# One core, linear attention and a gated layer: the same work in another hand-written order of all engines

## The chip, the core and the metric

The kernel runs on one core of one Trainium2 chip. Five engines work side by side, each through its own queue in order: TensorE (PE in the profile, its weight loads PEld), VectorE (DVE), ScalarE (ACT), GpSimd (POOL) and SyncE (SP, which here only issues DMAs). The metric is the device time of one execution in microseconds, as the median of several runs. The median of the kernel before is 104.37 us over 3 runs (104.37 to 105.62).

## The reference

Two stages. First, causal linear attention with decay `lam` per head, in blocks, for 4 batches, 8 heads, 768 positions and 64 channels. Its output is laid out as 3072 tokens by 512 features. Then a gated ("highway") layer on it:

```python
intra = einsum('bhic,bhjc->bhij', qb, kb) * Dmask      # Dmask: lam ** (i-j), causal
intra = einsum('bhij,bhjd->bhid', intra, vb)
inter = einsum('bhid,bhde->bhie', qb * lam_pow, kv_state)
out[:, :, sl] = intra + inter
kv_state = lam_block * kv_state + einsum('bhsd,bhse->bhde', kb * rev_pow, vb)
...
x = out.transpose(0, 2, 1, 3).reshape(B * S, H * D)
H = maximum(x @ w_h, 0); T = sigmoid(x @ w_t + b_t)
return T * H + (1 - T) * x
```

Inputs and output are float32.

## The kernel before

The kernel works in 12 super-blocks `n` of 256 positions, three to a batch. The decay is taken into the operands: q is multiplied by powers of `lam`, v by inverse powers, so that the mask is only 0 and 1 and the states simply add up within a batch. All products are in bf16.

The whole order is a list of tokens, `PLAN`, written out in the source. A loop reads it from left to right; each token calls one small function that issues the instructions of one step, and every engine's queue gets its instructions in the order in which the tokens stand. Semaphores between engines come from the data: a step waits for what it reads, and for the last readers of the buffer that it overwrites. `@` names the engine of a step, `=` the PSUM banks (seven, 0 to 6, and one for the state sums). The steps, with `n` the super-block, `b` one of its two halves of 128 positions, `e` the even or odd heads:

- `Lk`, `Lq`, `Lv`: load half of k, q or v (256 KB each, issued on SP, lines 221 and 224); `W.w.g`: half of a weight matrix (w=1 is the gate's `w_t`, w=0 `w_h`; line 235); `WC`: a quarter of it to bf16.
- `CK`: k to bf16 (tile kb). `CQ`: q times powers (qb, line 249). `CV`: v times powers (vs, line 255). A last number of 2 means both halves at once.
- `TK`, `TQ` (super-blocks 0 to 2, line 267) and `T.n` (from 3 on, 32 products, line 275): k and q turned by TensorE into PSUM. `EK`, `EQ`, `FK`, `FQ`: the copies of these to SBUF (kT, qT); a `T.n` is followed by four.
- `S.0`, `U.0.b`: scores and states of super-block 0 (lines 295, 300). `SS.n.e`: scores of the heads `e`, with states of the half `1-e` in between. `KE.n.b`: the copy of the state sums to SBUF (ss). The next states must wait for it.
- `M`: mask, from PSUM to SBUF (DVE, line 352), four for each n. `I`: queries times states (line 368). `A`: masked scores times v (line 374), into the same banks (bo). `D.n.b`: attention output to bf16 (xT), the input of the second stage.
- `BP`: the bias, copied into a bank ahead of the gate product. `F.n.b.1`: gate product (bt, line 404), `F.n.b.0`: the other product (bh, line 404); four matrix instructions each, called a block here. `TX.n`: xT turned back (bx, line 398). `G`: sigmoid (ACT, line 413). `X`: (gate - 1) times x (DVE, w, line 424). `H`: relu times gate (DVE, y, line 418). `Y`: total (ob, line 431). `ST`: store.
- `BS`, `B`, `BC`: the bias, split and broadcast. `PT`: ScalarE's table for the sigmoid (line 479). `Z`: an idle product of 256 columns that keeps TensorE busy at the start (line 461).

A copy is issued at line 113 on ScalarE and at line 115 on the others, whatever step it belongs to, so groups at these lines are told apart by their tiles. Buffers rotate: three for each of the loaded tiles, three or four for kb, qb, vs, kT, qT and ss, five for the output.

Of the kernel before, what the change touches and what calls it, by code (L numbers as in the profile page):

```python
# [27 lines left out]
G.1.0.2@ACT BP.1.1.2@DVE=3 TX.1.2=5 CK.3.2@ACT SS.2.1=26 KE.2.0@ACT M.2.1.1@DVE M.2.1.0@DVE F.0.0.1.2 BP.0.1.2@ACT=4
Lv.4.1 F.1.1.1.2 G.1.1.2@ACT Lq.5.1 Lv.4.0 Lk.5.0 CQ.3.2@POOL T.3=62 FQ.3.1@ACT FQ.3.0@ACT M.2.0.0@DVE WC.0.0.0@ACT
X.1.0.2@DVE WC.0.0.1@DVE I.2=13 A.2.1 A.2.0 F.0.1.1.2 Lq.5.0 FK.3.0@ACT FK.3.1@DVE CV.3.2@POOL SS.3.1=26 D.2.0@ACT  # L30
X.1.1.2@DVE WC.0.1.0@DVE BP.2.0.2@DVE=1 G.0.0.2@ACT WC.0.1.1@POOL F.1.1.0.2=5 F.1.0.0.2=0 KE.3.0@ACT D.2.1@ACT
M.3.1.0@DVE CQ.4.2@POOL TX.0.2=2 H.1.1.2@DVE Y.1.1.2@POOL H.1.0.2@DVE Y.1.0.2@DVE CK.4.2@POOL F.0.0.0.2=3 H.0.0.2@DVE
Lk.5.1 X.0.0.2@DVE BP.2.1.2@ACT=5 F.2.1.1.2 G.0.1.2@ACT G.2.1.2@ACT Lv.5.0 Lq.6.0 Lk.6.0 Y.0.0.2@POOL SS.3.0=40 Lq.6.1
M.3.1.1@DVE X.0.1.2@DVE CV.4.2@POOL T.4=35 CQ.5.2@POOL Lv.5.1 KE.3.1@ACT CK.5.2@POOL F.2.0.1.2 M.3.0.0@DVE FK.4.0@ACT
Lk.6.1 TX.2.2=6 Lq.8.0 M.3.0.1@DVE Lv.6.0 FK.4.1@ACT X.2.1.2@DVE FQ.4.1@ACT Lv.6.1 G.2.0.2@ACT X.2.0.2@DVE F.2.0.0.2=2
H.2.0.2@DVE I.3=40 A.3.1 Lq.7.0 FQ.4.0@ACT SS.4.1=51 M.4.1.0@DVE KE.4.0@ACT A.3.0 Y.2.0.2@POOL M.4.1.1@DVE
BP.3.1.2@ACT=2 F.0.1.0.2=3 H.0.1.2@DVE D.3.1@ACT F.2.1.0.2=6 H.2.1.2@DVE T.5=51 FQ.5.0@ACT Y.2.1.2@DVE Y.0.1.2@POOL
FK.5.0@ACT Lk.8.1 Lq.8.1 SS.4.0=03 FQ.5.1@ACT KE.4.1@ACT Lq.7.1 F.3.1.1.2 CK.6.2@ACT FK.5.1@DVE I.4=65 M.4.0.1@DVE
A.4.1 SS.5.0=13 M.4.0.0@DVE CQ.6.2@POOL D.3.0@ACT Lk.8.0 M.5.0.0@DVE A.4.0 D.4.0@DVE M.5.0.1@DVE D.4.1@ACT F.3.1.0.2=0
G.3.1.2@ACT H.3.1.2@DVE CV.5.2@POOL Lk.7.1 BP.3.0.2@ACT=4 CV.6.2@POOL TX.3.2=1 T.6=56 FQ.6.1@ACT SS.5.1=23 M.5.1.0@DVE  # L40
BP.4.0.2@ACT=0 F.3.0.1.2 FQ.6.0@DVE F.4.0.1.2 FK.6.1@ACT FK.6.0@DVE CQ.8.2@POOL KE.5.0@ACT G.4.0.2@ACT CQ.7.2@POOL
I.5=62 Lk.7.0 Lv.7.0 A.5.0 M.5.1.1@DVE A.5.1 SS.6.1=53 X.3.1.2@DVE G.3.0.2@ACT X.3.0.2@DVE CK.7.2@POOL M.6.1.0@DVE
F.3.0.0.2=0 H.3.0.2@DVE Lq.9.1 BP.4.1.2@ACT=4 F.4.1.1.2 M.6.1.1@DVE D.5.0@ACT KE.6.0@ACT SS.6.0=16 Y.3.1.2@POOL
D.5.1@DVE CK.8.2@ACT Lv.7.1 M.6.0.0@DVE T.8=50 G.4.1.2@ACT Lq.9.0 KE.6.1@ACT Lv.9.0 T.7=34 FK.7.1@ACT Lk.9.0
FK.7.0@ACT FK.8.1@ACT F.4.1.0.2=2 Lk.9.1 FQ.7.1@ACT FQ.7.0@DVE FQ.8.1@ACT F.4.0.0.2=1 M.6.0.1@DVE Lv.8.1 CV.7.2@POOL
H.4.1.2@DVE BP.5.1.2@ACT=2 TX.4.2=3 H.4.0.2@DVE X.4.0.2@DVE X.4.1.2@DVE I.6=64 Lv.8.0 A.6.0 Y.3.0.2@POOL FK.8.0@DVE
SS.7.1=10 M.7.1.1@DVE Y.4.1.2@POOL F.5.1.1.2 M.7.1.0@DVE ST.1 FQ.8.0@ACT F.5.1.0.2=3 Lk.10.0 G.5.1.2@ACT KE.7.0@ACT
H.5.1.2@DVE Lk.11.0 A.6.1 D.6.1@DVE SS.8.0=50 M.8.0.1@DVE M.8.0.0@DVE Lv.9.1 D.6.0@ACT SS.7.0=21 M.7.0.0@DVE
F.5.0.0.2=3 CK.9.2@POOL KE.7.1@DVE BP.5.0.2@ACT=6 F.5.0.1.2 Lq.10.0 BP.6.0.2@ACT=4 Lv.10.0 F.6.0.1.2 CQ.9.2@POOL
G.5.0.2@ACT Lq.10.1 BP.6.1.2@ACT=6 H.5.0.2@DVE Lk.10.1 G.6.0.2@ACT CV.8.2@POOL Y.4.0.2@POOL TX.5.2=0 X.5.1.2@DVE  # L50
Y.5.1.2@POOL T.9=52 FQ.9.1@ACT ST.4 Lv.10.1 FK.9.1@ACT SS.8.1=34 KE.8.0@ACT M.7.0.1@DVE FQ.9.0@DVE F.6.1.1.2
M.8.1.1@DVE CV.9.2@POOL F.6.1.0.2=1 M.8.1.0@DVE G.6.1.2@ACT H.6.1.2@DVE I.8=24 FK.9.0@ACT CQ.10.2@POOL I.7=63 A.7.0
A.7.1 A.8.1 SS.9.1=51 D.7.0@ACT X.5.0.2@DVE M.9.1.0@DVE Y.5.0.2@POOL KE.9.0@DVE A.8.0 D.7.1@ACT TX.6.2=0 X.6.1.2@DVE
F.6.0.0.2=6 M.9.1.1@DVE BP.7.0.2@ACT=3 F.7.0.1.2 D.8.0@ACT BP.7.1.2@ACT=2 TX.7.2=5 Lq.11.1 D.8.1@ACT BP.8.1.2@ACT=4
H.6.0.2@DVE G.7.0.2@ACT X.6.0.2@DVE X.7.0.2@DVE CK.10.2@POOL F.7.1.1.2 CV.10.2@POOL T.10=16 SS.9.0=03 FK.10.0@DVE
Lq.11.0 ST.0 FQ.10.0@ACT Y.6.1.2@POOL CQ.11.2@POOL G.7.1.2@ACT Y.6.0.2@POOL Lk.11.1 M.9.0.1@DVE F.8.1.1.2 KE.9.1@DVE
F.7.0.0.2=1 F.7.1.0.2=2 G.8.1.2@ACT M.9.0.0@DVE H.7.0.2@DVE I.9=34 H.7.1.2@DVE A.9.1 A.9.0 FQ.10.1@ACT X.7.1.2@DVE
FK.10.1@ACT SS.10.1=06 M.10.1.0@DVE F.8.1.0.2=1 D.9.1@ACT BP.9.1.2@ACT=2 ST.2 D.9.0@ACT KE.10.0@DVE F.9.1.1.2
BP.8.0.2@ACT=4 G.9.1.2@ACT H.8.1.2@DVE Lv.11.1 M.10.1.1@DVE SS.10.0=50 KE.10.1@ACT M.10.0.1@DVE CK.11.2@POOL T.11=31
FK.11.1@DVE FK.11.0@ACT Lv.11.0 CV.11.2@POOL Y.7.0.2@POOL FQ.11.1@ACT M.10.0.0@DVE ST.6 ST.5 TX.8.2=2 X.8.1.2@DVE  # L60
F.8.0.1.2 FQ.11.0@ACT Y.7.1.2@POOL I.10=60 G.8.0.2@ACT A.10.0 A.10.1 D.10.1@ACT X.8.0.2@DVE SS.11.0=15 M.11.0.0@DVE
D.10.0@ACT SS.11.1=34 BP.10.1.2@ACT=0 M.11.0.1@DVE M.11.1.1@DVE ST.3 TX.9.2=2 X.9.1.2@DVE Y.8.1.2@POOL BP.9.0.2@ACT=6
F.8.0.0.2=1 H.8.0.2@DVE Y.8.0.2@POOL M.11.1.0@DVE ST.7 F.9.1.0.2=5 F.9.0.1.2 G.9.0.2@ACT KE.11.0@ACT H.9.1.2@DVE
Y.9.1.2@DVE F.10.1.1.2 G.10.1.2@ACT TX.10.2=4 F.9.0.0.2=1 X.9.0.2@DVE I.11=36 A.11.1 A.11.0 BP.10.0.2@ACT=5
H.9.0.2@DVE Y.9.0.2@POOL ST.9 D.11.1@DVE F.10.0.1.2 G.10.0.2@ACT ST.8 X.10.1.2@DVE F.10.1.0.2=0 D.11.0@DVE
H.10.1.2@DVE X.10.0.2@DVE F.10.0.0.2=2 BP.11.0.2@ACT=1 F.11.0.1.2 G.11.0.2@ACT TX.11.0=6 H.10.0.2@DVE X.11.0.2@DVE
F.11.0.0.2=3 H.11.0.2@DVE BP.11.1.0@ACT=0 TX.11.1=4 Y.10.1.2@POOL BP.11.1.6@ACT=2 F.11.1.1.6 BP.11.1.5@DVE=5
# [452 lines left out]
```

## Time and profile before

| what | value |
|---|---|
| median of 3 runs | 104.37 us |
| profiled execution | 104.44 us, of which the span is 102.7 us |
| mean granted TensorE clock | 0.997 |
| read from HBM, written | 20.97 MB, 6.29 MB |
| loads of k, q, v on SP | 72, of 256 KB, median 5.5 to 5.7 us to landing |
| DMA shares of the span's 16 engines, main queue | 80.6% |
| longest waits of SP for totals, ahead of stores | 26.2 us in 5 |

The span runs from the first instruction to the last of one profiled execution; its own time has 1.7 us around it. DMA is full from about 2 to 60 us, and has room after that. The waits of SP for totals lie in the second half of the span, where few loads are left behind them.

### The profile page before, as it was taken

To read this page: it belongs to the slowest core of one execution; us is meant where nothing else is said; L and a number is where in the kernel's file an instruction comes from. 1 tells how busy PE (TensorE), PEld (TensorE's weight loads), DVE (VectorE), ACT (ScalarE), POOL (GpSimd) and SP (SyncE) were. 2 spreads that over 40 slices of the span, in tenths; PEclk is the share of its full clock that TensorE was granted. 3 is DMA by queue.
4 is the path that set the end of the run, shared out by engine and by line. 5 is a ranking of instruction groups with operands and counts; after the bars stand their busy time and mean duration, and the time that the engine had idled before them with its cause. 6 is when DMAs were issued, how large, how long until landed. Compare 5 with 4: busy or idle time off the path is not lost.

```text
span 102.7 us, 4320 instructions
## 1 busy us (share of the span) xinstructions
PE 90.0 (88%) x1834; PEld 58.5 (57%) x1853; DVE 86.2 (84%) x159; ACT 69.8 (68%) x125; POOL 76.7 (75%) x69
## 2 busy tenths in 40 slices
...
GB/s 18 259 316 352 361 372 382 377 348 387 351 347 351 284 293 339 318 337 328 293 265 358 345 344 105 6 206 288 343 341 59 238 374 208 10 0 198 211 286 125
DMA packets 33485, 27.54 MB, mean 268 GB/s; under 512 B 1465, under 2 KB 26425, under 8 KB 33466
## 3 DMA queue, kind: packets, MB, share of 16 engines
q1 hardware_dynamic: 33168, 27.14, 80.6%
...
HBM read 20.97 MB, written 6.29 MB: 265 GB/s over the span
## 4 chain that ended last, share of the span: by engine, by line
PE 66%; ACT 11%; DMA 6%; DVE 5%; SPq 4%; issue 3%; POOL 2%; ACTq 0%; POOLq 0%
PE bt L404 19%; PE bh L404 18%; PE bs L295 8%; DMA qf<-in_q_dram 6%; PE bx L398 5%; PE bo L374 5%; PE btr L275 5%; ACT kT L113 3%; ACT qT L113 3%; PE bo L368 3%; SPq L224 3%; PE kv L300 2%; POOL qb L249 2%; SPq L221 2%; DVE y L418 1%
## 5 line engine op out<-in xcount | busy, mean ns | idle before, releaser
L352 DVE TENSOR_TENSOR m<-bs,tri 128x512 bf16<-128x512 f32 x48 | 31.5, 684 | 2.7 <-PE bs L295 1.6
L431 POOL TENSOR_TENSOR ob<-y,w 128x512 f32<-128x512 bf16 (+1 forms) x21 | 23.7, 1136 | 10.3 <-DVE w L424 3.0
L404 PEld LDWEIGHTS <-xT 128*128 128x128 bf16 x208 | 18.0, 98 | 17.4
L255 POOL TENSOR_TENSOR vs<-vf,pow_v 128x1024 bf16<-128x1024 f32 (+1 forms) x12 | 22.0, 1836 | 7.8 <-DMA vf<-in_v_dram 7.8
L404 PE MATMUL bh<-w_b,xT 128*128 128x512 bf16 (+2 forms) x95 | 23.1, 361 | 0.7 <-issue 0.3
L404 PE MATMUL bt<-w_b,xT 128*128 128x512 bf16 (+2 forms) x94 | 22.7, 361 | 1.1 <-issue 0.8
L249 POOL TENSOR_TENSOR qb<-qf,pow_q 128x1024 bf16<-128x1024 f32 x11 | 20.9, 1907 | 3.0 <-DMA qf<-in_q_dram 3.0
L413 ACT ACTIVATE g<-bt 128x512 f32<-128x512 f32 (+2 forms) x26 | 14.5, 564 | 10.6 <-PE bt L404 10.3
L424 DVE SCALAR_TENSOR_TENSOR w<-g,bx 128x512 bf16<-128x512 f32 (+2 forms) x26 | 16.5, 640 | 1.9 <-ACT g L413 1.9
L295 PE MATMUL bs<-qT,kT 64*64 64x128 bf16 x384 | 14.2, 218 | 2.6 <-ACT qT L113 1.2
L418 DVE SCALAR_TENSOR_TENSOR y<-bh,g 128x512 bf16<-128x512 f32 (+1 forms) x21 | 14.1, 673 | 0.4 <-PE bh L404 0.2
L295 PEld LDWEIGHTS <-kT 64*64 64x64 bf16 x384 | 11.4, 106 | 5.3 <-issue 3.6
L113 ACT ACTIVATE bt<-b_bc 128x512 f32<-128x512 f32 (+2 forms) x22 | 12.5, 577 | 1.2 <-DVE y L418 1.0
L113 ACT ACTIVATE qT<-btr 128x512 bf16<-128x512 bf16 x15 | 8.7, 604 | 4.0 <-DVE kT L115 2.7
L113 ACT ACTIVATE xT<-bo 128x512 bf16<-128x512 f32 x16 | 9.4, 601 | 2.9 <-PE bo L374 2.9
L300 PE MATMUL kv<-vs,kb 64*64 64x64 bf16 x320 | 9.4, 197 | 0.8 <-ACT ss L113 0.7
L113 ACT ACTIVATE ss<-kv 128x512 bf16<-128x512 f32 x14 | 8.4, 601 | 1.6 <-PE bs L295 1.6
L374 PE MATMUL bo<-m,vs 64*64 64x128 bf16 x384 | 8.6, 219 | 0.7 <-DVE m L352 0.7
L300 PEld LDWEIGHTS <-kb 64*64 64x64 bf16 x320 | 7.6, 107 | 1.0 <-issue 0.9
L398 PEld LDWEIGHTS <-xT 128*128 128x128 bf16 x96 | 6.2, 98 | 2.9 <-issue 0.4
L374 PEld LDWEIGHTS <-vs 64*64 64x64 bf16 x384 | 6.3, 106 | 2.3 <-issue 1.1
L398 PE MATMUL bx<-id,xT 128*128 128x128 bf16 x96 | 7.5, 219 | 0.1
...
## 6 DMA issues: line engine op xcount, KB each, us to landing
...
```

The costliest lines, as they stand in the source:

```text
L113: A.activation(dst, src, AF.Copy)
L249: ENG[eng].tensor_tensor(new(("qb", n), [128, Q, 2, D])[:, :, es].rearrange("p j e d -> p e j d"), in0=get("qf", n)[:, es].rearrange("p e ...
L255: ENG[eng].tensor_tensor(new(("vs", n), [128, H, J, D])[:, heads(p)], in0=get("vf", n)[:, heads(p)].rearrange("p h (j d) -> p h j d", j=J) ...
L295: T.matmul(get("s", n, e, hp // 2)[half(b), hp % 2, j, :], lhsT=get("kT", n)[half(e), hp, j, half(b)], rhs=get("qT", n)[half(e), hp, b * C ...
L300: T.matmul(kv[half(e), hp, half(e)], lhsT=get("kb", n)[half(b), j, 2 * hp + e, :], rhs=get("vs", n)[half(b), 2 * hp + e, j, :], start=firs ...
L352: V.tensor_tensor(new(("m", n, e, u), [128, 2, J, C]), in0=get("s", n, e, u), in1=tri[:, None].to_broadcast([128, 2, J, C]), op=ALU.mult)
L374: T.matmul(get("o", n, b)[half(e), hp, :], lhsT=get("vs", n)[half(b), 2 * hp + e, j, :], rhs=get("m", n, e, hp // 2)[half(b), hp % 2, j, : ...
L398: T.transpose(t[:, i, j, :], get("xT", n)[:, j, b * C:(b + 1) * C], id128)
L404: T.matmul(t, lhsT=get("xT", n)[:, j, b * C:(b + 1) * C], rhs=w_b[w][:, j, z], start=(j == 0 and not w), stop=(j == KC - 1), skip_group_ch ...
L418: V.scalar_tensor_tensor(y, in0=get("h", n, b, p), scalar=0.0, in1=get("g", n, b)[:, z], op0=ALU.max, op1=ALU.mult)
L424: V.scalar_tensor_tensor(new(("w", n, b), [C, DM])[:, z], in0=get("g", n, b)[:, z], scalar=1.0, in1=x.rearrange("p j f -> p (j f)")[:, z], ...
L431: ENG[eng].tensor_tensor(o, in0=y, in1=get("w", n, b)[:, z], op=ALU.subtract)
```

## The change

Only `PLAN` is replaced: no function, no buffer count and no tile. The steps are the same, with two more `Z` (34 for 32). What is another: the order on every queue, the banks, and the engine of some steps. Counts by engine that differ:

| step | before | after |
|---|---|---|
| CQ, both halves | POOL 11 | POOL 10, DVE 1 |
| CV, both halves | POOL 11 | POOL 10, DVE 1 |
| CK, both halves | POOL 6, ACT 5 | POOL 5, ACT 6 |
| CK, one half | ACT 1, DVE 1 | ACT 2 |
| EK, both halves | ACT 2 | ACT 1, DVE 1 |
| EQ, one half | DVE 2 | DVE 1, ACT 1 |
| FK | ACT 12, DVE 6 | ACT 9, DVE 9 |
| FQ | ACT 15, DVE 3 | ACT 13, DVE 5 |
| KE | ACT 14, DVE 6 | ACT 16, DVE 4 |
| D | ACT 16, DVE 8 | ACT 19, DVE 5 |
| WC | POOL 5, DVE 2, ACT 1 | POOL 4, DVE 3, ACT 1 |
| BP, 512 wide | ACT 20, DVE 3 | ACT 19, DVE 4 |
| BP of quarter 5 of 11.1 | DVE | ACT |
| Y of 11.1, 256 wide / quarter 6 | POOL / DVE | DVE / POOL |

`U.0.0`, the first states, stands ahead of both `S.0` on TensorE. `TK.1.2` goes ahead of `TQ.1.2`. `T.7` and `T.8`, neighbours before, are apart; `T.10` and `T.9` are neighbours, in this order. The table load `PT` goes from ahead of the first k cast on ScalarE to between `D.0.1` and `EQ.2.2`. The diff, cut to the start, the part around the first gate products, the turns of 10 and 9, and the end:

```diff
-Z.1=0 Z.1=1 BS.0@DVE Z.1=2 Lk.1.0 Lv.0.0 Z.1=3 BS.1@DVE Z.1=4 BS.2@ACT Z.1=5 Z.1=6 Lq.0.1 Z.1=0 Lk.0.1 Z.1=1 Z.1=2
-Z.1=3 Lq.0.0 Lk.0.0 Z.1=4 Z.1=5 Lv.0.1 CV.0.1@POOL Z.1=6 Lq.1.1 Z.1=0 Z.1=1 Lq.1.0 CQ.1.2@POOL Z.1=2 Z.1=3 Lk.1.1
-Z.1=4 PT@ACT BS.3@DVE Z.1=5 CK.0.1@ACT Z.1=6 Z.1=0 TK.0.1=1 CQ.0.1@DVE CV.0.0@DVE Z.1=2 EK.0.1@ACT Z.1=3 CQ.0.0@DVE
-CK.0.0@DVE Lv.1.1 Lv.1.0 CV.1.2@POOL Z.1=4 TQ.0.2=5 EQ.0.1@DVE Z.1=6 Lq.2.0 Z.1=0 Z.1=2 Lk.2.0 TK.0.0=3 EQ.0.0@DVE
-Z.1=4 S.0.1=16 EK.0.0@ACT Lk.2.1 U.0.0 S.0.0=02 M.0.0.1@DVE M.0.1.1@DVE KE.0.0@DVE Z.1=4 Lq.2.1 CQ.2.2@POOL CK.1.2@ACT
-W.1.1 WC.1.1.1@POOL Z.1=3 Z.1=5 Lv.2.0 B=4 M.0.0.0@DVE TQ.1.2=3 I.0=15 W.1.0 Lv.2.1 Lq.3.0 M.0.1.0@DVE Lk.3.1
-EQ.1.2@ACT U.0.1 KE.0.1@DVE Lq.3.1 TK.1.2=6 EK.1.2@ACT A.0.0 A.0.1 SS.1.1=03 KE.1.0@ACT D.0.1@DVE CK.2.2@ACT Lk.3.0
-M.1.1.1@DVE M.1.1.0@DVE SS.1.0=26 Lv.3.1 WC.1.1.0@POOL Lv.3.0 TK.2.2=5 W.0.0 W.0.1 M.1.0.0@DVE D.0.0@DVE BC@ACT
-KE.1.1@ACT I.1=30 WC.1.0.0@POOL TQ.2.2=2 Lq.4.1 Lq.4.0 EK.2.2@ACT BP.1.0.2@ACT=4 WC.1.0.1@POOL A.1.0 M.1.0.1@DVE
-CV.2.2@POOL EQ.2.2@ACT A.1.1 D.1.0@ACT D.1.1@DVE SS.2.0=16 M.2.0.1@DVE Lk.4.0 BP.0.0.2@DVE=0 Lk.4.1 F.1.0.1.2
...
+Z.1=0 Z.1=1 Z.1=2 Z.1=3 Z.1=4 Z.1=5 Z.1=6 Z.1=0 Lk.1.0 Z.1=1 Lv.0.0 Lq.0.0 CV.0.0@POOL BS.0@ACT Lk.0.1 Z.1=2 Z.1=3
+Lk.0.0 Z.1=4 Z.1=5 Lq.0.1 CQ.0.0@DVE Z.1=6 Z.1=0 Lv.0.1 Z.1=1 Z.1=2 Lq.1.1 Lq.1.0 Z.1=3 BS.1@DVE CK.0.1@ACT BS.2@DVE
+BS.3@DVE Z.1=4 Z.1=5 Lk.1.1 CK.0.0@ACT Lv.1.1 Z.1=6 Lk.2.0 Z.1=0 Z.1=1 CK.1.2@POOL Z.1=2 TK.0.1=3 Z.1=4 Z.1=5 Z.1=6
+EK.0.1@ACT TK.0.0=0 EK.0.0@ACT Z.1=1 CQ.0.1@DVE TQ.0.2=2 EQ.0.0@ACT Z.1=4 Lv.1.0 Z.1=5 Z.1=6 CV.0.1@DVE U.0.0 S.0.0=31
+EQ.0.1@DVE Lk.2.1 S.0.1=04 Z.1=5 KE.0.0@DVE U.0.1 Lq.2.0 Lq.2.1 M.0.1.0@DVE Lv.2.1 TK.1.2=6 CQ.1.2@DVE Z.1=2 I.0=51
+KE.0.1@ACT W.1.0 W.1.1 Z.1=2 TQ.1.2=2 EK.1.2@ACT M.0.0.0@DVE EQ.1.2@ACT Lv.2.0 B=6 BC@ACT CV.1.2@DVE SS.1.1=32
+KE.1.0@ACT CK.2.2@POOL CQ.2.2@POOL M.0.1.1@DVE A.0.0 WC.1.0.0@POOL M.0.0.1@DVE M.1.1.1@DVE A.0.1 BP.0.0.2@ACT=6
+SS.1.0=40 TK.2.2=2 Lq.3.1 D.0.1@ACT TQ.2.2=1 PT@ACT WC.1.1.1@POOL M.1.1.0@DVE Lk.3.1 Lk.3.0 Lq.3.0 M.1.0.1@DVE W.0.0
+W.0.1 M.1.0.0@DVE EQ.2.2@ACT I.1=30 Lq.4.0 EK.2.2@DVE WC.1.1.0@DVE A.1.1 A.1.0 KE.1.1@DVE Lv.3.1 D.0.0@ACT D.1.0@ACT
+Lv.3.0 Lq.5.1 Lk.4.1 BP.1.0.2@DVE=5 SS.2.0=42 M.2.0.1@DVE M.2.0.0@DVE WC.1.0.1@POOL BP.1.1.2@ACT=3 F.0.0.1.2 F.1.0.1.2
...
+M.8.1.0@DVE D.7.0@ACT T.10=10 BP.7.0.2@ACT=6 FK.10.0@DVE T.9=25 FK.9.0@DVE F.7.0.1.2 F.6.0.0.2=3 FK.10.1@DVE
+FQ.9.1@ACT Lk.11.0 FK.9.1@ACT X.6.0.2@DVE FQ.10.1@ACT Y.5.1.2@POOL G.7.0.2@ACT FQ.10.0@ACT FQ.9.0@DVE H.6.0.2@DVE
+F.7.0.0.2=5 H.7.0.2@DVE X.6.1.2@DVE BP.7.1.2@ACT=6 SS.9.1=02 M.9.1.0@DVE KE.9.0@ACT F.7.1.1.2 G.7.1.2@ACT M.9.1.1@DVE
...
+Y.11.1.0@DVE F.11.1.0.6=1 F.11.1.1.5 G.11.1.5@ACT H.11.1.6@DVE X.11.1.6@DVE Y.11.1.6@POOL F.11.1.0.5=5 X.11.1.5@DVE
+ST.11.0.2 ST.11.1.0@ACT H.11.1.5@DVE Y.11.1.5@DVE ST.11.1.6 ST.11.1.5@ACT
```

More of the change, by code (lines that the diff above doesn't have):

```diff
@@ L28 @@
[L28 to L67, printed above, removed]
```

41 lines of the change are left out of this document (38 added, 3 removed).

## The prediction

> **What bounds the kernel now.** I read the page's busy shares first, then the same shares by stretch, then the chain of waits, then the timeline of the first 21 us, and last the groups by shape for prices.
>
> ```profile
> span 102.7 us, 4320 instructions
> PE 90.0 (88%) x1834; PEld 58.5 (57%) x1853; DVE 86.2 (84%) x159; ACT 69.8 (68%) x125; POOL 76.7 (75%) x69
> 11.46:24.00 12.54, 9.20 (x245) 6.85 (x245) 9.39 (x16) 8.64 (x12) 10.29 (x10) 1.00 1.10 370
> 24.00:96.00 72.00, 68.62 (x1486) 43.84 (x1501) 65.15 (x109) 54.06 (x101) 60.40 (x44) 1.00 0.80 262
> ```
>
> The last two rows are windows (span, then busy time of PE, weight load, DVE, ACT, POOL, then clock, DMA share, GB/s). From 24 to 96 us TensorE is busy 68.62 of 72 and VectorE 65.15: TensorE sets the pace, with 3.4 us idle, and VectorE is a close second with 6.9 idle. An order can win only TensorE's idle time there. From 11.46 to 24 us TensorE is idle 3.3 of 12.5 us while the DMA share is full: that is the fill.
>
> The chain of waits (start, length, what) shows what ends the fill:
>
> ```profile
> 5.53 6.05 DMA qf<-in_q_dram
> 11.71 1.91 POOL qb L249
> ...
> 17.76 1.05 ACT kb L113
> 18.81 0.49 ACT b_bc L113
> 19.29 0.49 ACT ss L113
> 19.78 0.91 ACT kT L113
> 20.70 0.49 ACT bt L113
> 21.19 0.95 ACT qT L113
> ...
> 22.18 0.63 PE bs L295 x16
> 22.81 0.54 PE bt L404 x2
> ```
>
> A load, a POOL multiply, and then from 17.76 to 22.14 one unbroken run of ScalarE work (4.4 us), behind which the scores of super-block 2 and the first gate product (bt, 22.81) start. After 22.81 the chain is mostly TensorE, apart from two heaps treated below. So there are three stretches to price: the time to the first gate product, the middle, and the tail.
>
> The change alters no matrix product except two more spins, so I cost it by these three.
>
> **The fill.** Where loads land, and what the DMA allows, is seen in waits on landings:
>
> ```profile
> 6.59 1.28 ACT L479 ACT_TABLE_LOAD   x1
> ...
> 10.46 1.04 POOL L255 TENSOR_TENSOR vs<-vf,pow_v 128x512 bf16<-128x512 f32 x1 [7.25 <-DMA vf<-in_v_dram]
> 12.43 1.06 ACT L113 ACTIVATE kb<-kf 128x1024 bf16<-128x1024 f32 x1 [1.08 <-DMA kf<-in_k_dram]
> 13.98 1.90 POOL L255 TENSOR_TENSOR vs<-vf,pow_v 128x1024 bf16<-128x1024 f32 x1 [0.37 <-DMA vf<-in_v_dram]
> 17.35 1.90 POOL L249 TENSOR_TENSOR qb<-qf,pow_q 128x1024 bf16<-128x1024 f32 x1 [1.47 <-DMA qf<-in_q_dram]
> 20.57 1.18 POOL L115 CAST w_b<-w_f 128x512 bf16<-128x512 f32 x2 [0.20 <-DMA w_f<-in_moe_w_t_dram]
> ```
>
> Below the first row, these are the 7th, 10th, 12th and 16th load and the second half of the gate weights. Loads land about (17.35-10.46)/9 = 0.77 us apart. The new order keeps the same kinds in places 7 to 10 of SyncE's queue, and the same bytes lie ahead of the second weight half, so it too lands at about 20.5. Only v of super-block 1 moves, from places 11 and 12 to 11 and 13: 13.98+0.77 = 14.75.
>
> Prices (mean ns of one) for the steps that change engine:
>
> ```profile
> L249 DVE TENSOR_TENSOR qb<-qf,pow_q 128x512 bf16<-128x512 f32 x2 | 1.4, 682 | 0.3 <-DMA qf<-in_q_dram 0.3
> L352 DVE TENSOR_TENSOR m<-bs,tri 128x512 bf16<-128x512 f32 x48 | 31.5, 684 | 2.7 <-PE bs L295 1.6 <-PE kv L300 0.8
> L115 DVE COPY kT<-btr 128x512 bf16<-128x512 bf16 x6 | 2.5, 419 | 0.8 <-ACT qT L113 0.8
> L115 DVE CAST xT<-bo 128x512 bf16<-128x512 f32 x8 | 5.5, 685 | 1.5 <-PE bo L374 1.5
> L115 DVE CAST w_b<-w_f 128x512 bf16<-128x512 f32 x2 | 1.1, 530 | 0.0
> L113 ACT ACTIVATE ss<-kv 128x512 bf16<-128x512 f32 x14 | 8.4, 601 | 1.6 <-PE bs L295 1.6
> L115 POOL CAST kb<-kf 128x1024 bf16<-128x1024 f32 x6 | 6.2, 1042 | 0.0
> L479 ACT ACT_TABLE_LOAD x1 | 1.3, 1283 | 0.0
> ```
>
> Follow VectorE in its new order. CV.0.1 starts on the 7th load, 10.46, and EQ.0.1 follows (0.67+0.69): 11.8. The states U.0.0 then run at about 11.2 to 11.8, as before, but now ahead of the scores. KE.0.0, M.0.1.0, CQ.1.2 (two halves' worth, 1.36), M.0.0.0, CV.1.2 (1.36, an estimate at the price of CQ) at about 0.65 a step back to back: 12.55, 13.2, 14.55, 15.2, 16.55. Compared with POOL, which had finished qb at 13.62, VectorE is later by 0.9 with qb; but the new PE queue has TK.1.2 ahead of TQ.1.2, so SS.1.1 waits for CV.1.2 and starts at 16.65, against 16.55 before. So the price of this swap is 0.1 us. What is queued behind it on VectorE: four masks of super-block 1 to 20.45, EK.2.2 (0.84) 21.3, a weight cast (0.53) 21.8, KE.1.1 22.5, BP.1.0 23.2. No step of that run waits, so any microsecond lost in it is paid in full.
>
> ScalarE's run of 4.4 us loses the cast of k2 (1.05, now POOL), the kT copy (0.91, now VectorE) and the state copy KE.1.1 (0.49 of chain), and the bias copy goes ahead of SS.1.1, whose wait covers it: -2.94. It gains D.0.1 (0.6) and the table load, which had lain in idle time at 6.6 us and now stands between D.0.1 and EQ.2.2 (1.28): +1.88. Net -1.06. TensorE's TQ.2.2 ends near 20.1 as before, because POOL's qb of super-block 2 still begins on the 16th load; EQ.2.2 runs 20.2 to 21.2, EK.2.2 ends 21.3, SS.2.0 runs 21.35 to 21.75. The first gate product also needs its weights: POOL's two casts still follow the landing and end near 21.75. So it starts at 21.9 against 22.81: 0.9 earlier, which is nearly all that the weights allow (22.81-21.75 = 1.06).
>
> Of that, 0.5 goes at once: the second gate product waits for BP.1.0 until 23.2, though TensorE is free at 22.75. At the end of SS.2.1 I get 24.7 (24.80 before), with two blocks of four products done rather than one and a transposed group.
>
> ```profile
> 23.78 0.45 PE bx L398 x8
> 63.17 1.73 PE bt L404 x8
> ```
>
> A block is 1.73/2 = 0.865, so this is 1.73-0.865-0.45 = 0.42 more work done: a lead of 0.1+0.42 = 0.5 us. Bounds: a lead of 0.95, if BP.1.0 costs nothing; a loss of 0.8, if VectorE's run slips by 1.3.
>
> **The middle.** VectorE as a whole gains CQ 1.36, CV 1.36, EK 0.84, a weight cast 0.53, three kT copies 1.26, two qT copies 1.37 and a bias copy 0.69, and loses two KE, three D and an EQ (6 x 0.685 = 4.11; these and the qT and bias copies go at the price of the xT row), and a half CK (0.42, at that of kT): 7.41-4.53 = +2.9, and some 0.2 less for smaller pieces, +2.7. All the big items, 4.1, lie before 22 us where it had idle time, so after that its load is no larger. POOL loses 5.4 (two multiplies of 1.90, a kb cast of 1.04 and a w_b cast of 0.59), all off the path. The covers of waits are what changes. In the old order the two heaps are:
>
> ```profile
> 40.00:46.00 6.00, 4.95 (x132) 3.47 (x133) 4.97 (x10) 4.82 (x9) 6.00 (x5) 1.00 1.05 333
> 54.00:60.00 6.00, 5.19 (x118) 3.33 (x115) 4.57 (x9) 3.41 (x8) 3.48 (x4) 1.00 1.10 353
> ```
>
> TensorE idles 1.05 and 0.81 there: 1.86 us that the new order can remove. The second heap is T.8 next to T.7, eight copies at once; the new order sets them three blocks and six shorter groups apart. Instead it has T.10 next to T.9, with three blocks (2.6 us) ahead of SS.9.1 while VectorE has three kT copies, one qT copy and one rest to do, 1.26+0.68+0.68 = 2.6: 0.4 lost, as hops are not in that. It leaves a single block (0.865) between the two halves of the scores of 3, 4 and 9, where the copy of the states (0.60 on ScalarE) must fit: 0.2 for 3 and 9, and 0.5 for 4, where a k cast of 1.05 stands ahead of the copy. SS.11.0 follows FQ.11.0 on VectorE behind a mask and a state copy: 0.7. Sum 0.2+0.2+0.5+0.4+0.7 = 2.0 against 1.86 removed: +0.1. Bounds: -2.5 (of the 3.4 idle, 0.9 stays in hops), +2.5 (each of the five at twice its price and half of 1.86 kept).
>
> **The tail.** The last masks and scores come earlier and F.10.0.1 ahead of TX.10; after the last product VectorE now does relu, then total, since the rest of that quarter goes before the product ends.
>
> ```profile
> 98.35 0.27 DVE y L418
> ...
> 99.17 0.20 DVE w L424
> 99.39 0.29 DVE ob L431
> ```
>
> That takes out the 0.20, and a total of 256 columns on VectorE instead of one of 128 puts back about 0.1: -0.1, between -0.3 and +0.4.
>
> **Sum.** -0.5+0.1-0.1 = -0.5. The profiled execution took 104.44 us (span 102.7 and 1.7 around it), so 103.9; the median of 104.37 lies 0.07 below it, which changes nothing at this accuracy.
>
> [...]
>
> ```profile
> 16.00:24.00 8.00, 5.13 (x147) 4.13 (x148) 5.62 (x9) 6.03 (x10) 6.45 (x7) 1.00 1.10 367
> L128 PE MATMUL cold<-blank 128*128 128x512 bf16 x4 | 1.9, 628 | 1.3 <-DVE blank L123 1.3
> ```
>
> TensorE idles 2.9 us of these 8 in pieces, and the granted clock stays 1.00; the first four products at the start took 1.9/4 = 0.47 each against 0.865/4 = 0.22 later. [...]
>
> **The rivals.**
> 1. VectorE becomes the bound (slower). Its load rises 86.2+2.7 = 88.9; if its idle time stays at 102.7-86.2 = 16.5, because the new fill uses VectorE in the same gaps and opens others later, the span is 105.4 and the time 107.1. For it: the run from 11.2 to 23.2 has no slack. Against: 4.1 of the load is put where it idled. It decides from the point where the second gate product starts after 23.8, not 23.2. Chance 0.20.
> 2. The waits go and none come (faster): -0.9 in the fill and -1.86 in the middle: 101.7. For it: the longest heap is taken apart. Against: five short covers stand in the order. Chance 0.14.
> 3. It trades waits evenly, and the states ahead of the scores do nothing, because TensorE's queue is in order and both wait for the 7th load's consumers: 104.4. Chance 0.14.
> 4. The clock falls in the fill: 103.9+3.4 = 107.3. Chance 0.02.
>
> My forecast, about 103.9, has 0.50.
>
> **The numbers.** One measurement of this kernel tells about 2% from no change, 102.3 to 106.5. Faster by more than that: rival 2, 0.14. Slower: nearly all of rival 1 and rival 4, 0.19. Within: 0.67. The range runs from 102.2 (it takes in the better half of the bounds) to 106.6 (most of the way to rival 1): about 0.1 left out on each side.
>
> **What would show it.** Right: the first bt product near 21.9, the second near 23.2 behind a bias copy on VectorE; SS.1.1 still near 16.6; no idle at T.7 and T.8; short waits on the state copy before SS.3.0, SS.4.0 and SS.9.0; VectorE's busy time near 88.9 and POOL's near 71.3. Wrong: the first bt product after 22.8, VectorE idle over 6.9 us from 24 to 96 with TensorE idle over 3.4, or a granted clock below 1.00 after the start.

## The result, and the profile after

The changed kernel takes 103.49 us (median of 20 runs, 102.32 to 106.2), the kernel before 104.86 us beside it (20 runs, 103.33 to 106.76). The ratio is 0.9886 with a 95% interval of 0.9846 to 0.9926. These times leave out disturbed runs. Of 104.4 to 104.9 us that is 0.8 to 1.6 us, where 0.5 was forecast. The profiled execution took 102.56 us, against 104.44 before.

The page of the changed kernel, first lines, and its windows for the same stretches as before (columns as in the prediction):

```profile
span 100.9 us, 4327 instructions
PE 90.9 (90%) x1837; PEld 58.3 (58%) x1855; DVE 87.5 (87%) x161; ACT 71.3 (71%) x127; POOL 72.5 (72%) x65
```

```profile
11.46:24.00 12.54, 10.71 (x266) 7.37 (x267) 11.10 (x17) 9.71 (x14) 9.36 (x8) 1.00 1.10 379
24.00:96.00 72.00, 69.77 (x1472) 44.30 (x1490) 67.04 (x114) 55.68 (x101) 58.17 (x42) 1.00 0.80 261
40.00:46.00 6.00, 5.67 (x135) 3.83 (x137) 5.19 (x10) 5.16 (x10) 6.00 (x5) 1.00 1.05 331
54.00:60.00 6.00, 5.65 (x159) 3.80 (x152) 5.25 (x10) 5.18 (x11) 4.59 (x5) 1.00 1.00 331
```

In the fill TensorE is 1.5 us busier (10.71 for 9.20). In the two old heaps its idle time falls from 1.05 and 0.81 us to 0.33 and 0.35. Now the chain of waits of the changed kernel in the fill (start, length, what):

```profile
11.30 5.41 DMA qf<-in_q_dram
...
16.85 1.91 POOL qb L249
...
18.80 0.64 PE bqtr L267 x8
...
19.46 1.02 ACT qT L113
...
20.86 0.61 ACT xT L113
...
21.50 0.61 ACT bt L113
...
22.13 1.02 PE bt L404 x4
```

The load of q of super-block 2, POOL's multiply and the turn are the same steps as before, and each comes earlier: the load lands at 16.71 (17.28 before), the multiply starts at 16.85 (17.35 before), the turn at 18.80 (19.76 before). The copy of q (EQ.2.2) stood at the end of ScalarE's run, at 21.08, 0.7 us after the end of the turn; now it starts 0.02 us after it, at 19.46. The first gate product, which this chain does not pass through, starts at 21.10 (22.81 before); its second matrix instruction comes only at 21.49, behind POOL's last weight cast. VectorE in the same stretch, from the timeline (start, length, step, count):

```profile
12.51 1.21 DVE L249 TENSOR_TENSOR qb<-qf,pow_q 128x1024 bf16<-128x1024 f32 x1
13.64 0.69 DVE L352 TENSOR_TENSOR m<-bs,tri 128x512 bf16<-128x512 f32 x1
14.24 1.22 DVE L255 TENSOR_TENSOR vs<-vf,pow_v 128x1024 bf16<-128x1024 f32 x1
15.37 3.68 DVE L352 TENSOR_TENSOR m<-bs,tri 128x512 bf16<-128x512 f32 x6
18.96 0.69 DVE L115 COPY kT<-bktr 128x1024 bf16<-128x1024 bf16 x1
...
21.01 0.69 DVE L115 COPY bt<-b_bc 128x512 f32<-128x512 f32 x1
```

Two steps back to back start 0.60 us apart though each is shown with 0.69: six masks take 3.68 from the first start to the last end, so (3.68-0.69)/5 = 0.60 each. The bias copy for the second gate product ends at 21.70, not at the 23.2 of the prediction.

From the first gate product to the end of the last product it is 75.7 us in both kernels (22.81 to 98.56, and 21.10 to 96.81). From the end of SS.2.1, where the prediction's fill ends, it is 73.76 us before (from 24.80) and 72.83 after (from 23.98). What TensorE waited for behind the first gate product, first before, then after (total, times, longest):

```profile
PE bt L404 <- issue: 0.8, 5, 0.2
PE bo L374 <- DVE m L352: 0.7, 1, 0.7
PE bs L295 <- DVE y L418: 0.6, 1, 0.6
PE bh L404 <- issue: 0.3, 2, 0.2
```

```profile
PE bs L295 <- ACT kT L113: 0.3, 1, 0.3
PE bh L404 <- DVE qT L115: 0.3, 1, 0.3
PE bt L404 <- ACT ss L113: 0.2, 1, 0.2
PE bh L404 <- issue: 0.2, 1, 0.2
```

The named waits fall from 1.3 to 0.8 us. The "issue" at line 404 comes in pieces of at most 0.2, one product each, and the two traces hold 189 and 190 of the 208 products of that line: these look like missing records, not waits. The end, from the chain of the changed kernel:

```profile
96.37 0.24 PE bt L404 x4
...
96.63 0.29 ACT g L413
...
96.92 0.28 DVE y L418
97.20 0.39 DVE w L424 x2
97.59 0.22 DVE bh L418
...
97.84 0.29 DVE ob L431
```

On VectorE the rests of two quarters (w, x2) still stand ahead of the last relu and total. From the last product to the end of the span it is 4.05 us, 4.18 before.

### The profile page after: what moved, and what is told of

Read it like the earlier page. It is cut to its first block, busy times and chain, and to the rows that moved or that the text cites. A ratio compares the mean times of both kernels' runs of the same rounds, so it can differ in the third digit from the quotient of the medians.

```text
span 100.9 us, 4327 instructions
## 1 busy us (share of the span) xinstructions
PE 90.9 (90%) x1837; PEld 58.3 (58%) x1855; DVE 87.5 (87%) x161; ACT 71.3 (71%) x127; POOL 72.5 (72%) x65
## 4 chain that ended last, share of the span: by engine, by line
PE 58%; ACT 10%; SPq 10%; DVE 8%; DMA 5%; issue 4%; POOL 2%; DVEq 0%; POOLq 0%
PE bt L404 18%; PE bh L404 16%; SPq L224 7%; PE bs L295 7%; DMA qf<-in_q_dram 5%; PE bx L398 5%; PE bo L374 4%; PE bo L368 3%; SPq L221 3%; ACT qT L113 3%; ACT kT L113 2%; PE btr L275 2%; DVE qT L115 2%; POOL qb L249 2%; PE kv L300 2%
## 5 line engine op out<-in xcount | busy, mean ns | idle before, releaser
L404 PEld LDWEIGHTS <-xT 128*128 128x128 bf16 x208 | 18.1, 97 | 18.2 <-issue 0.8
L404 PE MATMUL bt<-w_b,xT 128*128 128x512 bf16 (+2 forms) x97 | 24.0, 362 | 0.5 <-ACT ss L113 0.2
L255 POOL TENSOR_TENSOR vs<-vf,pow_v 128x1024 bf16<-128x1024 f32 (+1 forms) x11 | 20.0, 1827 | 4.7 <-DMA vf<-in_v_dram 2.6
L249 POOL TENSOR_TENSOR qb<-qf,pow_q 128x1024 bf16<-128x1024 f32 x10 | 19.0, 1905 | 0.7 <-DMA qf<-in_q_dram 0.5
L295 PE MATMUL bs<-qT,kT 64*64 64x128 bf16 x384 | 15.0, 218 | 1.4 <-ACT qT L113 0.4
L113 ACT ACTIVATE xT<-bo 128x512 bf16<-128x512 f32 x19 | 10.8, 594 | 1.8 <-PE bo L374 1.7
L113 ACT ACTIVATE ss<-kv 128x512 bf16<-128x512 f32 x16 | 9.5, 596 | 3.4 <-PE kv L300 1.9
L115 POOL CAST kb<-kf 128x1024 bf16<-128x1024 f32 x5 | 6.1, 1225 | 7.0 <-DMA kf<-in_k_dram 7.0
L113 ACT ACTIVATE qT<-btr 128x512 bf16<-128x512 bf16 x13 | 7.6, 598 | 3.1 <-DVE kT L115 1.6
L113 ACT ACTIVATE kb<-kf 128x1024 bf16<-128x1024 f32 (+1 forms) x8 | 7.6, 946 | 1.5 <-DMA kf<-in_k_dram 1.4
```

What stands on the lines that cost most here:

```text
L113: A.activation(dst, src, AF.Copy)
L249: ENG[eng].tensor_tensor(new(("qb", n), [128, Q, 2, D])[:, :, es].rearrange("p j e d -> p e j d"), in0=get("qf", n)[:, es].rearrange("p e ...
L255: ENG[eng].tensor_tensor(new(("vs", n), [128, H, J, D])[:, heads(p)], in0=get("vf", n)[:, heads(p)].rearrange("p h (j d) -> p h j d", j=J) ...
L295: T.matmul(get("s", n, e, hp // 2)[half(b), hp % 2, j, :], lhsT=get("kT", n)[half(e), hp, j, half(b)], rhs=get("qT", n)[half(e), hp, b * C ...
L404: T.matmul(t, lhsT=get("xT", n)[:, j, b * C:(b + 1) * C], rhs=w_b[w][:, j, z], start=(j == 0 and not w), stop=(j == KC - 1), skip_group_ch ...
```

## The experiments

All ratios are to the kernel before, run beside. SS.2.0 and the first gate product are the two marks of the fill; they stand at 22.18 and 22.81 in the profile before, and at 20.54 and 21.10 after.

**1. The new fill with the old rest.** The new order through SS.2.0, less three bias copies, then what was left of the old order. The loads behind that point follow the old list.

```diff
-Z.1=0 Z.1=1 BS.0@DVE Z.1=2 Lk.1.0 Lv.0.0
...
+Z.1=0 Z.1=1 Z.1=2 Z.1=3 Z.1=4 Z.1=5 Z.1=6
...
+Lk.4.1 SS.2.0=16 Lq.4.1 BP.1.0.2@ACT=4
```

> The new order up to and including SS.2.0 (without its three bias copies, SS.2.0 in banks 1 and 6), then the old order of all that is left. Theory 'the fill does it': the first gate product near 21.2 us (22.8 before, 21.1 in the changed kernel) and the span near 101.2 (102.7 before, 100.9 in the changed kernel), ratio about 0.986. Rival 'the middle does it' (the two heaps near 42 and 56 us removed): the first gate product earlier, but the lead is lost at the old heaps, and the span stays near 102.5.

106.87 us (4 runs), ratio 1.0143 (1.0021 to 1.0266). At the seam some gate products come to other banks than in either order, and probably lose part of the copied bias there (not looked into); no instruction is left out, and the time can be read. The chain of this run shows what went wrong with it as a test:

```profile
22.96 6.77 DMA vf<-in_v_dram
...
29.87 1.91 POOL vs L255
```

SS.2.0 came at 21.20, earlier than before, but the mixed list asks for v of super-block 3 so late that SS.3.0 started about 4 us later (38.05 for 33.96): TensorE stood 1.57 us for that v, and from 32.4 us on the granted clock was 0.50 for 3.41 us. This priced the seam, not the fill; 5 mends it.

**2. The old fill with the new rest.** The old order through SS.2.0 (less the bias copies that the new rest has itself), then what is left of the new one.

```diff
-Z.1=0 Z.1=1 Z.1=2 Z.1=3 Z.1=4 Z.1=5 Z.1=6
...
+Z.1=0 Z.1=1 BS.0@DVE Z.1=2 Lk.1.0 Lv.0.0
...
```

> The old order up to and including SS.2.0 (without BP.1.0, SS.2.0 in banks 4 and 2), then the new order of all that is left. Theory 'the fill does it': first gate product near 22.8 and a span near 102.6, ratio 0.998 to 1.003. Rival 'the middle does it': span near 101.0, ratio about 0.985.

104.7 us (10 runs), ratio 0.995 (0.9876 to 1.0024); the bias is as in 1. The first gate product came at 22.27 and the last product ended 76.3 us later, of which 0.94 is a piece in which nothing was waited for (last section). Without it the new rest takes 75.4, 0.3 us less than the old one. The ratio puts its gain alone at 0.5%, in an interval that reaches from nothing to all of the change's 1.1%.

**3 and 4. The load order.** In the profile after, loads landed up to 1.1 us earlier than before, and the 5th and 6th load are exchanged between the two orders. 3 makes that exchange in the old kernel, 4 undoes it in the new one.

```diff
-Z.1=3 Lq.0.0 Lk.0.0 Z.1=4
+Z.1=3 Lk.0.0 Lq.0.0 Z.1=4
```

> The kernel before with the 5th and 6th load exchanged (k before q, so that the first loads of super-block 0 stand q k k q as in the changed kernel, where they stood q k q k). Theory 'where the fifth load stands makes all later loads land 1.1 us sooner': the 8th load lands near 9.9 us instead of 10.9, POOL's CQ.1.2 starts near 10.7 instead of 11.7, and the first gate product moves up by 0.3 to 1.0. Rival 'the gap before the fifth landing is chance of one execution': landings as in the kernel before or scattered, no change in the span beyond 0.3.

```diff
-Lk.0.0 Z.1=4 Z.1=5 Lq.0.1 CQ.0.0@DVE
+Lq.0.1 Z.1=4 Z.1=5 Lk.0.0 CQ.0.0@DVE
```

> The changed kernel with the 5th and 6th load exchanged (q before k, the old pattern q k q k). Theory 'the place of the fifth load': the 8th load lands near 10.9 instead of 9.85, SS.1.1 starts near 16.5 instead of 15.5, the first gate product near 21.9 (what was forecast with the old landings) instead of 21.1, span up by 0.5 to 1.0. Rival 'chance': as the changed kernel, within 0.3.

3: 104.37 us (10 runs), ratio 0.998 (0.9927 to 1.0033): nothing. 4: 104.39 us (4 runs), ratio 0.99 (0.977 to 1.0029). The half of k that landed at 12.34 before and 11.22 after landed at 11.36 in 3, at 11.67 in 4, and at 11.17 in 2, which has the old order. So the gap is the luck of an execution, and the 1.7 us lead of the profiled pair is partly that luck. Both runs showed something else. Two windows of 4, and two groups of its turns on TensorE:

```profile
13.66:17.07 3.41, 2.54 (x64) 1.53 (x62) 3.41 (x6) 2.80 (x4) 2.24 (x2) 1.00 1.07 382
18.00:20.00 2.00, 2.00 (x37) 1.83 (x30) 1.62 (x4) 1.76 (x2) 1.32 (x3) 0.50 1.09 372
```

```profile
18.62 1.04 PE L267 MATMUL bktr<-id,kb 128*128 128x128 bf16 x8
19.45 1.06 PE L267 MATMUL bqtr<-id,qb 128*128 128x128 bf16 x8
```

The granted clock is 0.50 from 17.1 us on, for 3.41 us, and eight turns take 1.04 instead of 0.62. The profile of 3, the old order, has the same from 19.4 us.

**5. The new fill with the old rest, mended.** As 1, with the old rest's banks renamed to fit the seam (SS.2.0=42 among them), and the loads from the 21st on in the old order.

```diff
-Lk.4.1 SS.2.0=16 Lq.4.1 BP.1.0.2@ACT=4
...
-G.1.0.2@ACT BP.1.1.2@DVE=3 TX.1.2=5 CK.3.2@ACT SS.2.1=26
+SS.2.0=42 Lk.4.1 BP.1.0.2@ACT=6
...
+G.1.0.2@ACT BP.1.1.2@DVE=3 TX.1.2=5 CK.3.2@ACT SS.2.1=12
```

> As e1, with the seam mended: the new order up to and including SS.2.0 (without three bias copies), then the old order, its banks renamed so that each step finds the same kind of bank as it did, and the loads from the 21st on in the old order. Theory 'the fill does it': first gate product near 21.3 us, 75.8 us from there to the last product as in the kernel before, span near 101.3. Rival 'the middle does it': from the first gate product to the last more than 76.8 us, span 102.3 or more.

104.54 us (10 runs), ratio 0.9986 (0.9926 to 1.0046). SS.2.0 came at 20.52, as in the changed kernel, but the lead was gone at once. Its chain:

```profile
20.56 0.75 POOL w_b L115
...
21.38 0.61 POOL w_b L115
21.99 1.87 POOL vs L255
...
23.91 0.19 PE kv L300
```

The second half of the gate weights landed at 20.51 (19.95 in the changed kernel), its casts and the multiply of v of super-block 2 follow on POOL, and the old order wants that v next: TensorE waited 0.84 us for the casts and 0.25 for v, SS.2.1 ended at 24.54 (24.80 before), and from the first gate product, at 22.00, it took 76.7 us to the last, of which 0.49 is a piece without a cause that is shown. The theory that the fill alone does it fell: the interval leaves out the change's 0.9886. That of 2 does not quite.

**6. ScalarE's run put back.** The k cast, the kT copy and the state copy return to ScalarE in the changed kernel.

```diff
-CK.2.2@POOL ... EK.2.2@DVE ... KE.1.1@DVE
+CK.2.2@ACT ... EK.2.2@ACT ... KE.1.1@ACT
```

> The changed kernel with three steps of the fill given back to ScalarE (cast of k2, the kT copy EK.2.2 and the state copy KE.1.1, which the change had put on GpSimd and VectorE). Theory 'ScalarE's run ended the fill, and taking 2.9 us out of it is the gain': EQ.2.2 begins near 20.5 instead of 19.5, SS.2.0 starts near 22.4 instead of 20.5, the first gate product near 22.9 instead of 21.1, span near 102.5, ratio about 1.00 to the kernel before. Rival 'the loads end the new fill anyway': SS.2.0 moves by less than 0.5 and the span stays within 0.5 of 100.9.

106.88 us (4 runs), ratio 1.0253 (1.0168 to 1.0338). Its ScalarE in the fill:

```profile
17.14 1.05 ACT L113 ACTIVATE kb<-kf 128x1024 bf16<-128x1024 f32 x1
...
19.21 1.28 ACT L479 ACT_TABLE_LOAD   x1
20.50 1.02 ACT L113 ACTIVATE qT<-bqtr 128x1024 bf16<-128x1024 bf16 x1
...
22.33 0.60 ACT L113 ACTIVATE ss<-kv 128x512 bf16<-128x512 f32 x1
```

The copy of q starts at 20.50 and the first gate product at 23.48, where 20.5 and 22.9 were expected. So these three steps on ScalarE, put back, hold the fill. The mean clock of its profiled run was 0.852; only starts in the fill are read from it, and of the whole price of 3 to 4 us only the sign and these steps are safe.

**7. Scores ahead of the states again.**

```diff
-U.0.0 S.0.0=31 EQ.0.1@DVE Lk.2.1 S.0.1=04
+S.0.0=31 EQ.0.1@DVE Lk.2.1 S.0.1=04 U.0.0
```

> The changed kernel with the first states U.0.0 behind both first scores again. Theory 'the place of the first states matters little, since SS.1.1 and later the q load of super-block 2 are waited for anyway': KE.0.0 about 0.5 later, SS.1.1 up to 0.5 later, SS.2.0 and the span within 0.3 of the changed kernel. Rival 'states first is what starts VectorE's run sooner': all steps of that run and the first gate product 0.5 later, span 101.4.

105.22 us (10 runs), ratio 1.0031 (0.997 to 1.0093): the gain is gone. VectorE's multiply CQ.1.2 started at 13.62 instead of 12.51, SS.1.1 at 16.62, and the first gate product at 22.46. Its first scores start 0.26 later than in the changed kernel (10.99 for 10.73), which the order of the two does not touch; the state copy KE.0.0, which heads VectorE's run, starts 1.09 later (12.41 for 11.32). So the order is worth some 0.8 us at that copy. In 8 of its 10 executions the mean clock was 0.983 or lower, so how much of the lost gain is the order's is not shown.

**8 and 9. More idle products in the fill.** 12 and 6 more `Z`, between 13 and 19 us.

```diff
-TQ.1.2=2 ... SS.1.1=32 ... A.0.1 ... TQ.2.2=1
+Z.2=2 TQ.1.2=2 ... Z.3=3 SS.1.1=32 ... Z.2=4 A.0.1 ... Z.5=1 TQ.2.2=1
```

> The changed kernel with twelve more idle products in the gaps of TensorE between 13 and 19 us (2 ahead of TQ.1.2, 3 ahead of SS.1.1, 2 ahead of A.0.1, 5 ahead of TQ.2.2). In the profiles of two earlier kernels the granted clock was 0.50 for 3.4 us from about 17 and 19 us on. Theory 'too little TensorE work in the stretch before lets the clock fall, in some executions': the clock stays at 1.00 in the fill in all or nearly all executions, the median of the kernel's times comes down by up to 1 us from 103.5 towards 102.8, and SS.2.0 stays within 0.2 of 20.5. Rival 'the fall does not depend on such work': mean clocks near 0.98 as often as before, median 103.5 or a little more by the products' own time (at most 0.3).

> The changed kernel with six more idle products (2 ahead of SS.1.1, 2 ahead of A.0.1, 2 ahead of TQ.2.2) in place of the twelve. Theory 'the clock falls for want of work in one window, and twelve kept it up but stood 0.5 us in the way': the clock stays at 1.00 in most executions, TQ.2.2 starts within 0.15 of the end of CQ.2.2, SS.2.0 near 20.6 plus what the loads land later, median near 102.9, below the changed kernel by 0.5 or more. Rival 'six are too few': mean clocks near 0.98 in as many executions as without them, median as the changed kernel.

8: 103.5 us (12 runs), ratio 0.994 (0.9888 to 0.9991). Mean clock 0.99 or higher in all 12 executions; in the changed kernel 9 of 20 are at 0.984 or lower. But five of the idle products and late scores stood ahead of the turn of q, which started at 19.38, not 18.80. It steadies the clock and gains nothing in the median. 9: 104.43 us (6 runs), ratio 0.9895 (0.9753 to 1.0036), with a lowered clock in 2 of 6: six are too few to tell.

**10. The changed kernel once more**, beside 9 and 11, and **11. idle products in the kernel before** (16 of them, from 16 to 22 us).

> The changed kernel itself, once more, beside the others on the same chip. Both theories: median 103.5, ratio to the kernel before 0.985 to 0.993; mean clocks near 0.98 in about half of the executions.

```diff
-SS.1.1=03 ... SS.1.0=26 ... TK.2.2=5 ... SS.2.0=16
+Z.3=0 SS.1.1=03 ... Z.4=2 SS.1.0=26 ... Z.1=5 TK.2.2=5 ... Z.8=1 SS.2.0=16
```

> The kernel before with sixteen more idle products in the gaps of TensorE between 16 and 22 us (3 ahead of SS.1.1, 4 ahead of SS.1.0, 1 ahead of TK.2.2, 8 ahead of SS.2.0). Theory 'the clock is a cost apart from the order': the clock stays up, the median falls by 0.5 to 1.0 below the kernel before, to near 103.8, and stays above the changed kernel with spins by 0.8 to 1.2, which is the order's own share. Rival 'the change gains by the clock': the two kernels with spins come out within 0.3 of each other.

10: 103.52 us (6 runs), ratio 0.9867 (0.9778 to 0.9956), though its profiled execution had the clock at 0.50 from 17.8 to 21.3 us and its first gate product only at 22.84. 11: 105.43 us (12 runs), ratio 1.0027 (0.997 to 1.0083). In 4 of these 12 the mean clock is still below 0.988, so 11 does not part its two theories; these idle products only brought no gain. What parts them is the median of the executions with a mean clock of at least 0.988, and of the rest: before 103.91 and 105.10 (36 and 40 executions beside the runs of this study), changed 102.76 and 104.97 (11 and 9). Where the clock is not lowered the change gains 1.15 us, so the clock is not where the gain comes from. The lowered clock goes with 1.2 us in the old order and 2.2 in the new; the second is loose, as the five lowered ones of 10 have a median of 103.78.

**12. v of super-block 1 back on POOL**, since in several profiles, where VectorE's multiply and POOL's k cast met, one of the two was longer (1.98 us for 1.04, 1.74 for 1.22; last section).

```diff
-CV.1.2@DVE SS.1.1=32
+CV.1.2@POOL SS.1.1=32
```

> The changed kernel with one step back on its old engine: v times powers of super-block 1 (both halves) on POOL instead of VectorE. In the profiles of the changed kernel and its variants this VectorE multiply and POOL's cast of k of super-block 2 start within a few tenths of each other, and one of the two is longer than elsewhere: the cast 1.98 and 2.01 us instead of 1.04 (the changed kernel, and the one with the 5th and 6th load exchanged), or the multiply 1.74 and 1.80 instead of 1.22 (the changed kernel again, and the one with the scores first). Theory 'they block each other': with both on POOL no such row is left (cast 1.04, every POOL multiply 1.90), v is ready at 15.5 (landing 13.5 + 1.9 + hops), the scores of super-block 1 start at 15.6, within 0.1 of the profiled changed kernel and some 0.5 earlier than where the multiply lost; VectorE's masks of super-block 1 come 0.6 to 1.1 earlier. The path of the fill is the load of q of super-block 2 and does not move, so the time is 103.0 to 103.7, ratio to the kernel before 0.982 to 0.990. Rival 'POOL has no room': multiply, cast and multiply in a row on POOL end after 18.75, each tenth is paid at the turn of q2, and the time is 103.8 to 104.4, ratio 0.990 to 0.996. Rival 'the long rows are something else': a POOL row of about 2.0 for the cast, or of over 2.5 for a multiply, shows up again though VectorE multiplies nothing at that time.

104.27 us (6 runs), ratio 0.9851 (0.9751 to 0.995): not to be told from the changed kernel. POOL in its profile:

```profile
13.86 1.90 POOL L255 TENSOR_TENSOR vs<-vf,pow_v 128x1024 bf16<-128x1024 f32 x1 [1.27 <-DMA vf<-in_v_dram]
15.70 1.04 POOL L115 CAST kb<-kf 128x1024 bf16<-128x1024 f32 x1
17.18 1.90 POOL L249 TENSOR_TENSOR qb<-qf,pow_q 128x1024 bf16<-128x1024 f32 x1 [0.44 <-DMA qf<-in_q_dram]
```

Every row has its usual length, and POOL still waits 0.44 for q: there was room. Its profiled span of 104.6 us has a piece of 1.50 us in which TensorE waited for nothing that is shown, and one of 1.29 of which the chain leaves 0.40 without a cause. No version beat the changed kernel by more than the scatter.

## Why the prediction was right, point by point

**The direction, and what bound the fill: right.** In the old order ScalarE's run ends the fill, whenever q lands. POOL's multiply of q and ScalarE's copy of it in 2, then in 11, both with the clock at 1.00 there:

```profile
15.60 1.90 POOL L249 TENSOR_TENSOR qb<-qf,pow_q 128x1024 bf16<-128x1024 f32 x1 [0.83 <-DMA qf<-in_q_dram]
20.19 1.05 ACT L113 ACTIVATE qT<-bqtr 128x1024 bf16<-128x1024 bf16 x1
```

```profile
16.00 1.90 POOL L249 TENSOR_TENSOR qb<-qf,pow_q 128x1024 bf16<-128x1024 f32 x1 [0.85 <-DMA qf<-in_q_dram]
20.63 1.04 ACT L113 ACTIVATE qT<-bqtr 128x1024 bf16<-128x1024 bf16 x1
```

q was multiplied at 17.50 and 17.90, and the copy still came 2.7 us later, with ScalarE busy without a break from the state copy KE.1.0 on. From that copy's start it is 3.82 us in 11 and in the profile before (17.26 to 21.08), and 3.30 in 2, which has one bias copy less there. In the new order the load ends the fill: SS.2.0 starts 3.83 us after q lands in the changed kernel (16.71 to 20.54) and in 12 (17.04 to 20.87), and 3.82 after it in 5 (16.70 to 20.52). Three steps put back on ScalarE (6) make it longer again.

**The size of the fill: near, by a path that was mis-sized.** The prediction's fill ends with SS.2.1, at a lead of 0.5 that counts 0.42 of work done earlier. SS.2.1 ended at 23.98 (24.80 before): a lead of 0.82+0.42 = 1.24 in the profiled pair. Much of that is luck: SS.2.1 ended at 24.34 in 11, in the old order, and at 24.74 in 12, in the new one, where the weights landed at 20.71 (19.95 in the changed kernel). The gain of the medians (104.86-103.49 = 1.4, or 1.15 where the clock is not lowered), less what the middle and the tail brought (below), leaves some 0.5 to 0.8 for the fill, an estimate. The step that was mis-sized is "Follow VectorE in its new order ... about 0.65 a step", down to "BP.1.0 23.2" and "0.5 goes at once". The price was taken from the mean duration (684 ns), but where steps follow back to back what counts is from start to start: 0.60, and 1.13 for the two big multiplies that were priced at 1.36 (12.51 to 13.64, 14.24 to 15.37). Over the run that is about 1.2 us. The run also began 0.6 earlier, and it did wait, 0.33 us for the weights. So the bias copy ended at 21.70, and the second gate product waited for nothing on VectorE. (The list has six masks, not four, ahead of EK.2.2; the time to 20.45 counts six.)

**TQ.2.2 "ends near 20.1 as before":** it ended at 19.44, and at 20.37 before. In the old order the turn of k ahead of it on TensorE waited for the k cast on ScalarE, so that it started 0.51 after POOL's multiply was done (19.25 to 19.76); the new order takes that wait away too.

**SS.1.1 "at 16.65, against 16.55 before":** it started at 15.52, for two of the reasons above: the price of a step, and landings that came earlier in this execution.

**The middle at +0.1: wrong, and both terms too large.** From the end of SS.2.1 to the last product it is 0.93 us shorter (72.83 for 73.76). 0.42 of that is the work done earlier, so the middle gained about 0.5. This is not the luck of a pair: less the pieces without a cause that is shown, that stretch is 73.8 (before), 73.8 (3), 73.7 (5) and 73.4 (11) with the old rest, and 72.8 (after), 72.9 (2), 72.7 (4), 72.8 (7), 73.0 (8), 72.9 (9) and 72.8 (10) with the new one; 1 (clock 0.50 for 3.41 us), 6 (mean clock 0.852) and 12 (the piece of 1.29) are not in this list. Of the "1.86 us that the new order can remove" 1.3 were named waits, and they are gone. The step that failed is the price of the five short covers, 2.0 us together; none cost anything: SS.3.0, SS.4.0, SS.9.1, SS.9.0 and SS.11.0 all start without a gap on TensorE. The 0.8 of named waits that came lie elsewhere (32.45, 55.53 and 60.25 us; the last, 0.16, is as long as the pieces that look like missing records). That the first gate product stands 75.7 us ahead of the last in both kernels hides this, because in the new order it starts before its weights are all there. That TensorE is busy 1.1 us longer from there on over the same products (73.4 for 72.3) is in part records that the old trace lacks; the rest is open.

**Fill and middle together.** With -0.5 for the middle in place of +0.1 the forecast would have been -1.1, close to what was measured; the middle's covers are the step that cost most. The stated range (102.2 to 106.6) would have held no change at all as well. Alone, the new rest has a ratio of 0.995 (2), which fits the 0.5 us of the traces; the new fill alone has 0.9986 (5). There it runs into the old rest, which wants v of super-block 2 before POOL has multiplied it, where the new rest puts a second gate block. In that profile the weights also landed 0.56 later, so how much of the loss is the order's is not shown, nor, within these intervals, that the two parts gain more together than their sum.

**The tail at -0.1: the size is right by luck (4.18 to 4.05), the reason is not.** The prediction had the rest X done before the last product, "so only" relu and total after it. The chain above shows two rests of 0.39 together on VectorE behind the sigmoid. From the last product to VectorE's last end it is 1.32 us instead of 1.12; what comes behind that, the store, is shorter by 0.3 (2.73 for 3.06). 1 and 5, which end in the old order, have 4.02 and 4.03 too, so the 0.13 is not the tail's order.

**VectorE as the bound (rival 1): fell.** It is busy 87.5 us, not 88.9, and from 24 to 96 us it idles 4.96 instead of 6.85 while TensorE idles less: more load did not make it the bound. POOL came to 72.5 (71.3 forecast).

**"The states ahead of the scores do nothing" (rival 3): fell.** In 7, without them, the copy KE.0.0, which heads VectorE's run in the fill, comes some 0.8 us later, because the states free it. The gain of the median is gone in 7 too, but the clock was low in most of its executions.

**The clock (rival 4, 2%): underrated.** The profiles of 3, 4 and 10 have a fall to 0.50 for 3.41 us. In the 3.41 us ahead of it the longest idle piece of TensorE in 4 is 0.36; from 16 to 18 us TensorE idles 1.16 in 3 (fall at 19.4) and 0.78 in 10 (fall at 17.8), all pieces together. A mean clock below 0.988 was seen in about half of the executions of both kernels (40 of 76 before, 9 of 20 changed), and goes with 1.2 to 2.2 us. No run shows the 3.4 us of rival 4; those 1.2 to 2.2 are what the runs showed in its place. The lowered clock was in the times of before too, so it left the sign alone.
